# One token load ahead of two transposing DMAs, the last scales later, one copy ahead of a square

## The chip, the cores and the metric

The kernel runs on one core of one Trainium2 chip. The metric is the device time of one execution in microseconds (us), of which a profiled execution also gives the span from the first to the last instruction. Five engines work side by side, each through its own instructions in order: TensorE (PE, matmuls; PEld its weight loads), VectorE (DVE), ScalarE (ACT), GpSimd (POOL) and SyncE (SP, which here only issues DMAs).

## The reference

Attention over 4 batches, 8 heads, 576 tokens and 64 features (four heads with a plain window of 32, four with a dilated one), then two dense layers over its 2304 tokens:

```python
h = x @ w_in                      # 2304x512 @ 512x2048
y = (h - tanh(h)) @ w_out         # -> 2304x512

h = y @ w_in2                     # 2304x512 @ 512x1024
e = exp(h - max(h, axis=-1))
solu = h * (e / (sum(e) + 1e-9))
mu, var = mean(solu), mean((solu - mu) ** 2)
out = ((solu - mu) / sqrt(var + 1e-6) * g_ln) @ w_out2     # 1024 -> 512
```

All of it is in float32; the kernel forms products from a high and a low half of each operand.

## The kernel before

The program has three parts. Attention and the first dense layer go first, in groups of 384 tokens. The first layer's output y goes to a DRAM buffer `y_dr`. The second layer, which all of the change concerns, reads it back in nine **pairs** (0 to 8) of 256 tokens, that is 18 **tiles** of 128 tokens: pair p has tiles 2p and 2p+1, and the odd one is finished first.

For each pair, `load_y(j)` (L636) loads y from DRAM into a buffer `yr`; SP issues it. There are two buffers of this kind, one that the even pairs 2, 4, 6, 8 take in turn and one for the odd pairs from 3 on. `split_y` makes PE's input of it, in parts: part "r" scales `yr` in place on ACT (L644) with `ysc`, part "s" makes sums and differences of quarters on POOL (L652), and parts 0, 2 and 1 round to float16 (on DVE at L664, or on ACT at L662 where `act=True`) and leave the remainder to POOL (L665).

`mm3(i)` is the first product of pair i, put together from seven block products of 6 matmuls each (`prod`, L749, a scheme with fewer block products than the plain one): "b11", "t2", "t1", "t3", "t4", "b21", "b22", in this order, in four PSUM banks. ACT copies the first bank to `c` (L781). DVE adds the second bank and `c` to `u2` (L784), the fourth bank and `u2` to `u3` (L792), and `neg_add` (L764) makes the scaled, negated h with a running minimum. "t4" is written into the second bank, so it waits until `u2` is made; "b21" goes into the fourth bank, so it waits for `u3`. `softmax_e` (L820, ACT) takes the exponential, `softmax_u` (L825) and `softmax_z` (L831, L832) on DVE make the product and take off the mean, `square` (L841, ACT) and `fac` (L846, L847, POOL) give the factor of the tile. `split_z` rounds to float16 (L869, ACT) and takes the remainder (L870, DVE); a transposing DMA (L874, issued by SP) turns the result, for tiles 1 and 17 PE does it (`trz`). `mm4` is the second product, 24 matmuls for a tile (L897); its result is scaled on ACT (L900) and stored (L901). `rest`, `rest1` and `rest2` make the scale that L900 needs.

PE's order is mm3(0), mm3(1), mm4 of tiles 1 and 0, mm3(2), mm4 of tiles 3 and 2, mm3(3) and so on: the work of ACT, DVE and POOL on pair i goes on while PE does mm4 of pair i-1. What is issued when is written out by hand: `mm3` calls functions that are given to it (`mid`) at four places, and `first` to `fourth` are those of pairs 1 and 2. All engines take their instructions in the order in which these lines are called.

`y_scale(k)` makes the scales of three pairs at a time from the maxima `ym`. For k = 0 and 1 it runs within the first layer; `y_scale(2, ...)` gives the scales of pairs 6, 7 and 8, its second half is `scale2`, called in `fourth`.

Of the kernel before, what the change touches and what calls it, by code (L numbers as in the profile page):

```python
# [14 lines left out]
ALU = mybir.AluOpType  # L15
# [25 lines left out]
def tile_kernel(ctx: ExitStack, tc: tile.TileContext, qk, vw, cst, w_in, w_out, w_in2, w_out2, g_ln, out):  # L41
    nc = tc.nc
# [38 lines left out]
    wsc = const.tile([128, 8], F32, name="wsc")  # L81
# [170 lines left out]
    def y_scale(k, pool, tag):  # L252

        d = ysc[:, k]
        m = ym[:, 2 * k:2 * k + 2]
        ps = spread(m, pool, tag, f"ysp{k}")

        def far():
            nc.vector.tensor_reduce(out=m, in_=ps, axis=mybir.AxisListType.X, op=ALU.max)

        def then():
            if k < 2:
                far()
            for c, a, b in ((0, 0, 0), (1, 0, 1), (2, 1, 1)):
                nc.vector.tensor_scalar(out=d[:, 0, c:c + 1], in0=m[:, a:a + 1], scalar1=m[:, b:b + 1], scalar2=2.0 ** -100,
                                        op0=ALU.max, op1=ALU.max)
            nc.vector.reciprocal(out=d[:, 1], in_=d[:, 0])
            nc.vector.tensor_scalar(out=d[:, 1], in0=d[:, 1], scalar1=2.0 ** 13, scalar2=None, op0=ALU.mult)
            nc.vector.tensor_scalar(out=d[:, 2], in0=d[:, 0], scalar1=wsc[:, 3:4], scalar2=-(2.0 ** -16), op0=ALU.mult,
                                    op1=ALU.mult)  # L270
        return then if k < 2 else (far, then)

# [359 lines left out]
    def load_y(j):  # L632
        if j < NP:
            pool = p3 if j > 2 and j % 2 else p2
            y_raw[j] = pool.tile([128, KD, YT], F32, tag="yr", name=f"yr{j}", bufs=1)
            nc.sync.dma_start(out=y_raw[j], in_=y_dr[:, :, j * YT:(j + 1) * YT])  # L636

    def split_y(j, parts=range(3), act=False):

        if j >= NP:  # L640
            return
        r = y_raw[j]
        if "r" in parts:
            nc.scalar.activation(out=r, in_=r, func=AF.Copy, scale=ysc[:, j // 3, 1, j % 3:j % 3 + 1])  # L644
        if 0 in parts:
            yt[j] = p2.tile([128, 2, 7, 2, TT], F16, tag="yt", name=f"yt{j}")
        if 0 in parts and j not in y_sm or "s" in parts:
            sm = y_sm[j] = p2.tile([128, 3, 2, TT], F32, tag="ysm", name=f"ysm{j}", bufs=1)
            a11, a21, a22 = r[:, 0:2, 0:TT], r[:, 0:2, TT:YT], r[:, 2:4, TT:YT]
            for o, a, b, op in ((sm[:, 0], a21, a22, ALU.add), (sm[:, 1], sm[:, 0], a11, ALU.subtract),  # L650
                                (sm[:, 2], a11, a21, ALU.subtract), (a21, r[:, 2:4, 0:TT], sm[:, 1], ALU.subtract)):
                nc.gpsimd.tensor_tensor(out=o, in0=a, in1=b, op=op)  # L652
        if not set(parts) & {0, 1, 2}:
            return
        y, sm = yt[j], y_sm[j]
        yh = y[:, 0].rearrange("p s k t -> p (s k) t")
        yl = y[:, 1].rearrange("p s k t -> p (s k) t")
        for p, sl, v in ((0, slice(0, 4), r[:, :, 0:TT]), (2, slice(4, 8), r[:, :, TT:YT]),
                         (1, slice(8, 14), sm.rearrange("p s k t -> p (s k) t"))):
            if p in parts:  # L660
                if act:
                    nc.scalar.copy(out=yh[:, sl], in_=v)  # L662
                else:
                    nc.vector.tensor_copy(out=yh[:, sl], in_=v)  # L664
                nc.gpsimd.tensor_tensor(out=yl[:, sl], in0=v, in1=yh[:, sl], op=ALU.subtract)  # L665
        if 2 in parts:
            y_raw.pop(j)
            y_sm.pop(j)
# [84 lines left out]
    def bank(pool, tag, i, nm):  # L753
        return pool.tile([128, 512], F32, tag=tag, name=f"s{nm}_{i}")
# [12 lines left out]
    def mm3(i, mid=()):  # L767

        y = yt.pop(i)
        sm = sml[i] = p3.tile([128, 2, 8], F32, tag="sml", name=f"sml{i}", bufs=3)  # L770
        for t in range(2):
            st[2 * i + t] = dict(sml=sm[:, t])
        mid = dict(mid)
        b0, b1 = bank(sa, "b0", i, "p1"), bank(sa, "b1", i, "p6")
        prod(b0, y, 0, "b11")
        prod(b1, y, 5, "t2")
        u2 = p3.tile([128, 512], F32, tag="u2", name=f"u2_{i}", bufs=1)
        u3 = p3.tile([128, 512], F32, tag="u3", name=f"u3_{i}", bufs=1)
        b2, b3 = bank(sb, "b2", i, "p5"), bank(sb, "b3", i, "p7")
        c = p3.tile([128, 512], F32, tag="c", name=f"c_{i}", bufs=1)  # L780
        nc.scalar.copy(out=c, in_=b0)  # L781
        if i > 0:
            split_y(i + 2, ("r",))
        nc.vector.tensor_tensor(out=u2, in0=b1, in1=c, op=ALU.add)  # L784
        if i > 2:
            split_y(i + 1, (1, 2))
            load_y(i + 3)
        prod(b2, y, 4, "t1")
        if 0 in mid:
            mid[0]()  # L790
        prod(b3, y, 6, "t3")
        nc.vector.tensor_tensor(out=u3, in0=b3, in1=u2, op=ALU.add)  # L792
        neg_add(i, 1, 1, b2, u3)
        b1 = bank(sa, "b1", i, "p4")
        prod(b1, y, 3, "t4")
        neg_add(i, 1, 0, b1, u3)
        if 1 in mid:
            mid[1]()
        softmax_e(2 * i + 1)
        b3 = bank(sb, "b3", i, "p2")  # L800
        prod(b3, y, 1, "b21")
        neg_add(i, 0, 0, b3, c)
        softmax_u(2 * i + 1)
        if 2 in mid:
            mid[2]()
        prod(b2, y, 2, "b22", first=False)
        neg_add(i, 0, 1, b2, u2)
        if 3 in mid:
            mid[3]()
        softmax_e(2 * i)  # L810
        softmax_z(2 * i + 1)
        square(2 * i + 1)
        fac(2 * i + 1)
        softmax_u(2 * i)
        softmax_z(2 * i)

# [20 lines left out]
    def square(i):  # L837

        d = st[i]
        d["f"], d["g"] = d["sml"][:, 4:5], d["sml"][:, 6:7]  # L840
        nc.scalar.activation(out=d["e"], in_=d["hn"], func=AF.Square, accum_out=d["sml"][:, 5:6])  # L841

    def fac(i):

        sc, var = (st[i]["sml"][:, c:c + 1] for c in (4, 5))
        nc.gpsimd.tensor_scalar(out=var, in0=var, scalar1=2.0 ** -20 / FF2, scalar2=1e-37, op0=ALU.mult, op1=ALU.max)  # L846
        nc.gpsimd.tensor_tensor(out=sc, in0=var, in1=half, op=ALU.pow)  # L847
# [12 lines left out]
    def rest2(p):  # L860
        ssum, sc, var, g = (sml[p][:, :, c] for c in (1, 4, 5, 6))
        nc.vector.tensor_tensor(out=var, in0=var, in1=sc, op=ALU.mult)
        nc.vector.scalar_tensor_tensor(out=g, in0=ssum, scalar=wsc[:, 6:7], in1=var, op0=ALU.mult, op1=ALU.mult)  # L863

    def split_z(i, dma=True):

        d = st[i]
        ab = d["ab"] = d["e"].bitcast(F16).rearrange("p (a n) -> p a n", a=2)
        nc.scalar.activation(out=ab[:, 0], in_=d["hn"], func=AF.Copy, scale=d["f"])  # L869
        nc.vector.scalar_tensor_tensor(out=ab[:, 1], in0=d["hn"], scalar=d["f"], in1=ab[:, 0], op0=ALU.mult,  # L870
                                       op1=ALU.subtract)
        t = d["zt"] = p3.tile([128, 2, NF2, TT], F16, tag="zt", name=f"zt{i}", bufs=4)
        if dma:
            nc.sync.dma_start_transpose(out=t.rearrange("p a j t -> p (a j) t"), in_=ab.rearrange("p a n -> p (a n)"))  # L874
# [29 lines left out]
    y_rows(2)  # L904
    split_y(2, ("r", "s"))
    mm3(0)
    far, scale2 = y_scale(2, zo, "zp")
    far()
# [12 lines left out]
    def third():  # L921
        rest2(0)
        split_y(2, act=True)

    def fourth():
        rest2(1)
        scale2()
        split_y(3, act=True)
        load_y(5)

    mm3(1, {0: first, 1: second, 3: third})
    for i in range(NP):
        o, e = 2 * i + 3, 2 * i + 2
        last = i + 2 == NP
        if i + 1 < NP:
            square(e)
            fac(e)
            split_z(o, not last)
            if i > 0:
                rest(i + 1)  # L940
            split_z(e)
            if i > 0:
                split_y(i + 3, (0,))
                rest1(i + 1)
            if last:
                rest2(i + 1)
            if i == 0:
                load_y(4)
        mm4(2 * i + 1)
        mm4(2 * i, (lambda: trz(o)) if last else None)  # L950
        if i == 0:
            mm3(2, {0: lambda: split_y(3, ("s",)), 1: lambda: (rest(1), rest1(1)), 3: fourth})
        elif i + 2 < NP:
            mm3(i + 2, {3: lambda: rest2(i + 1)})
# [77 lines left out]
```

## Time and profile before

| | us |
|---|---|
| median of 3 runs | 701.3 (699.94 to 701.52) |
| profiled execution | 700.27 |
| its span | 698.5 |
| PE busy | 673.4 |
| DVE busy | 501.3 |
| ACT busy | 384.2 |
| POOL busy | 172.9 |

PE is the engine that works nearly all the time. The others have much free time on the whole, so the place of their waits matters and not their sum. In the rows below a line of a timeline gives the start and the duration in us, the engine, the line of the kernel, the operation, what it writes and reads with shapes, and how many instructions are merged in it; in brackets stands how long the engine stood idle just before, and what ended that.

### The profile page before, as it was taken

The page shows a single profiled execution, that of the slowest core. Times are in us where ns is not written, and L with a number is a line of the kernel's source. Part 1 is how long each engine was busy: PE and PEld are TensorE (multiplying, and loading weights), DVE is VectorE, ACT ScalarE, POOL GpSimd, SP SyncE. Part 2 cuts the span into 40 slices and gives each one's busy share as a digit, 9 for nine tenths or more (in the row PEclk, how much of TensorE's full clock was granted, in tenths as well). Part 3 has the DMA queues.
Part 4 walks back from the last instruction along what each step waited for, and adds up shares of the span by engine and source line. Part 5 has one row for each costly group of instructions (what it writes and reads, how often), then busy time and mean ns, then how long its engine had stood idle before and what let it go on. Part 6 is the DMA issues. An engine that isn't in the chain of part 4 may idle for free. (4 is left out here: it accounts for less than half of the span.)

```text
span 698.5 us, 11389 instructions
## 1 busy us (share of the span) xinstructions
PE 673.4 (96%) x4010; PEld 558.9 (80%) x4010; DVE 501.3 (72%) x1257; ACT 384.2 (55%) x917; POOL 172.9 (25%) x174
## 2 busy tenths in 40 slices
PE   6898999999999999999999999999999969999997
PEld 5687899999999999999999999999944424444443
DVE  5987667477767876787777743599978577777751
ACT  5778776455555555455555533475657345555442
POOL 2312311101110111101111010365225456545410
PEclk9999999999999999999999999999999989999999
DMA  9975641242334332342213001453311554433243
GB/s 281 349 252 177 192 123 23 95 143 90 116 121 139 103 115 91 121 155 87 82 53 114 2 1 60 165 178 134 114 46 30 131 140 103 80 97 78 70 88 92
DMA packets 68009, 80.82 MB, mean 116 GB/s; under 512 B 36592, under 2 KB 52464, under 8 KB 67952
## 3 DMA queue, kind: packets, MB, share of 16 engines
q1 hardware_dynamic: 64784, 75.37, 36.6%
q10 hardware_dynamic: 3168, 4.72, 1.8%
q8 instruction: 32, 0.52, 0.3%
q14 instruction: 25, 0.20, 0.1%
HBM read 62.25 MB, written 9.44 MB: 103 GB/s over the span
## 5 line engine op out<-in xcount | busy, mean ns | idle before, releaser
L458 PE MATMUL h<-x,wi 128*128 128x384 f32 x1152 | 221.8, 342 | 1.1 <-DVE t L469 1.1
L485 PE MATMUL y<-gs,wo 128*128 128x384 f32 x1152 | 217.7, 339 | 0.0
L458 PEld LDWEIGHTS h<-x,wi 128*128 128x128 f32 x1152 | 199.7, 190 | 2.4 <-DVE t L469 1.3
L485 PEld LDWEIGHTS y<-gs,wo 128*128 128x128 f32 x1152 | 199.6, 189 | 1.8
L357 POOL TENSOR_TENSOR p<-p,rs 96x512 f32<-96x512 f32 x47 | 57.5, 1222 | 352.2 <-DVE rs L355 307.6
L475 DVE TENSOR_TENSOR gs<-t,gs 128x384 fp32r<-128x384 f32 x96 | 81.4, 848 | 24.3 <-ACT gs L472 24.2
L469 DVE TENSOR_TENSOR t<-h,t 128x384 f32<-128x384 f32 x96 | 53.0, 552 | 63.0 <-ACT t L466 62.8
L897 PE MATMUL po<-w2o_o,zt 128*128 128x512 f16 x432 | 95.1, 379 | 0.6 <-DVE zt L886 0.6
L466 ACT ACTIVATE t<-h 128x384 f32<-128x384 f32 x96 | 46.8, 488 | 82.8 <-PE h L458 79.3
L349 ACT ACTIVATE p<-p,nm 96x128 f32<-96x128 f32 x192 | 75.0, 393 | 21.2 <-DVE nm L314 20.8
L472 ACT CAST gs<-t 128x384 fp32r<-128x384 f32 x96 | 48.9, 510 | 63.8 <-DVE t L469 63.6
L897 PEld LDWEIGHTS <-zt 128*128 128x128 f16 x432 | 42.1, 98 | 51.8 <-DVE zt L886 1.1
L749 PEld LDWEIGHTS <-yt 128*128 128x128 f16 x378 | 37.4, 99 | 53.8 <-issue 11.3
L749 PE MATMUL sp<-w2i_t,yt 128*128 128x512 f16 x216 | 49.8, 386 | 7.7 <-DVE u L784 7.7
L820 ACT ACTIVATE e<-hn,sml 128x1024 f32<-128x1024 f32 x18 | 20.7, 1148 | 53.8 <-DVE sml L764 40.6
L870 DVE SCALAR_TENSOR_TENSOR e<-hn,sml,e 128x1024 f16<-128x1024 f32 x18 | 25.6, 1425 | 19.0 <-ACT e L869 19.0
L749 PE MATMUL sp<-w2i_b,yt 128*128 128x512 f16 x162 | 38.7, 384 | 0.0
L309 PE MATMUL qkp<-qkr 64*96 64x128 f32 x160 | 29.4, 339 | 7.1 <-DMA qkr<-in_qk_dram 5.4
L349 ACT ACTIVATION_READ_ACCUMULATOR p<-p,nm 96x1 f32 x192 | 36.2, 189 | 0.0
L309 PEld LDWEIGHTS qkp<-qkr 64*96 64x96 f32 x160 | 24.1, 205 | 11.7 <-DMA qkr<-in_qk_dram 5.7
L396 DVE TENSOR_TENSOR x<-pv,x 128x384 fp32r<-128x384 f32 x24 | 16.2, 697 | 20.2 <-ACT x L394 19.8
L364 PE MATMUL tp<-cst_sb,p 96*128 96x96 f32 x192 | 27.0, 268 | 3.4 <-POOL p L357 2.4
(111 smaller groups left out, 825.2 us busy)
## 6 DMA issues: line engine op xcount, KB each, us to landing
qkr<-in_qk_dram SPq DMA_DIRECT2D x28, 448.0 KB, 3.4
raw_wi<-in_w_in_dram SPq DMA_DIRECT2D x16, 511.8 KB, 7.1
raw_wo<-in_w_out_dram SPq DMA_DIRECT2D x16, 511.8 KB, 7.3
v<-in_vw_dram SPq DMA_DIRECT2D x48, 128.0 KB, 3.4
y_dr<-ys ACTq DMA_DIRECT2D x6, 768.0 KB, 3.9
yr<-y_dr SPq DMA_DIRECT2D x9, 512.0 KB, 5.1
out_dram<-o SPq DMA_DIRECT2D x18, 256.0 KB, 2.7
qkr<-in_qk_dram SPq DMA_DIRECT2D x20, 224.0 KB, 5.3
```

What stands on the lines that cost most here:

```text
L309: nc.tensor.matmul(ps[:, b], d["r"][:64, b * NQ:(b + 1) * NQ], d["r"][:64, QC + b * NK:QC + (b + 1) * NK], start=True, stop=True)
L349: nc.scalar.activation(out=d["p"][:, b], in_=d["p"][:, b], func=AF.Exp, scale=-1.0, bias=d["nm"][:, b:b + 1], accum_out=d["sm"][:, b:b + 1])
L357: eng.tensor_tensor(out=d["p"], in0=d["p"], in1=d["rs"].unsqueeze(2).to_broadcast([NQ, 4, NK]), op=ALU.mult)
L364: nc.tensor.transpose(ps[:NK, b * NQ:(b + 1) * NQ], d["p"][:, b], ident[:NQ, :NQ])
L458: nc.tensor.matmul(ps, w[:, a, k * 128:(k + 1) * 128], xt[g, k][:, b], start=(n == 0), stop=(n == 3 * KD - 1))
L466: nc.scalar.activation(out=t, in_=ps, func=AF.Tanh)
L469: nc.vector.tensor_tensor(out=t, in0=ps, in1=t, op=ALU.subtract)
L472: nc.scalar.copy(out=gs[:, 0], in_=t)
L475: nc.vector.tensor_tensor(out=gs[:, 1], in0=t, in1=gs[:, 0].bitcast(F32), op=ALU.subtract)
L485: nc.tensor.matmul(yb[g][m], wo[c][:, a, m * 128:(m + 1) * 128], gs[:, b], start=(c == 0 and i == 0), stop=(c == NF - 1 and i == 2))
L749: nc.tensor.matmul(ps, y[:, a, blk, kk], w2i[w, kk][:, b], start=first and q == 0, stop=q == 5, skip_group_check=not first)
L897: nc.tensor.matmul(po, z[:, a, j], w2o[j][:, b], start=(q == 0), stop=(q == 3 * NF2 - 1))
```

## The change

`load_y(4)` is called ahead of the two `split_z` of pair 1 in place of behind them. `y_scale` makes its nine values with four DVE instructions in place of six, and `scale2` moves from `fourth` (in mm3(2)) to the place behind `rest1(2)`. In mm3(0) `square(1)` and `fac(1)` fall away at the end, and mm3(1) calls them behind its copy to `c`; the scaling of y of pair 3, which stood there, moves to the end of `third`. For the last pair `rest2(8)` moves behind `trz(17)`.

```diff
@@ y_scale
         def then():
             if k < 2:
                 far()
-            for c, a, b in ((0, 0, 0), (1, 0, 1), (2, 1, 1)):
-                nc.vector.tensor_scalar(out=d[:, 0, c:c + 1], in0=m[:, a:a + 1], scalar1=m[:, b:b + 1], scalar2=2.0 ** -100,
-                                        op0=ALU.max, op1=ALU.max)
+            nc.vector.tensor_scalar(out=d[:, 0, 0:3:2], in0=m, scalar1=2.0 ** -100, scalar2=2.0 ** -13, op0=ALU.max,
+                                    op1=ALU.mult)
+            nc.vector.tensor_tensor(out=d[:, 0, 1:2], in0=d[:, 0, 0:1], in1=d[:, 0, 2:3], op=ALU.max)
             nc.vector.reciprocal(out=d[:, 1], in_=d[:, 0])
-            nc.vector.tensor_scalar(out=d[:, 1], in0=d[:, 1], scalar1=2.0 ** 13, scalar2=None, op0=ALU.mult)
-            nc.vector.tensor_scalar(out=d[:, 2], in0=d[:, 0], scalar1=wsc[:, 3:4], scalar2=-(2.0 ** -16), op0=ALU.mult,
+            nc.vector.tensor_scalar(out=d[:, 2], in0=d[:, 0], scalar1=wsc[:, 3:4], scalar2=-(2.0 ** -3), op0=ALU.mult,
                                     op1=ALU.mult)
@@ mm3
         nc.scalar.copy(out=c, in_=b0)
-        if i > 0:
+        if i == 1:
+            square(1)
+            fac(1)
+        if i > 1:
             split_y(i + 2, ("r",))
...
         softmax_e(2 * i)
         softmax_z(2 * i + 1)
-        square(2 * i + 1)
-        fac(2 * i + 1)
+        if i > 0:
+            square(2 * i + 1)
+            fac(2 * i + 1)
@@ the order of the second layer
     def third():
         rest2(0)
         split_y(2, act=True)
+        split_y(3, ("r",))
 
     def fourth():
         rest2(1)
-        scale2()
         split_y(3, act=True)
         load_y(5)
...
             square(e)
             fac(e)
+            if i == 0:
+                load_y(4)
             split_z(o, not last)
             if i > 0:
                 rest(i + 1)
@@
                 split_y(i + 3, (0,))
                 rest1(i + 1)
-            if last:
-                rest2(i + 1)
-            if i == 0:
-                load_y(4)
+            if i == 1:
+                scale2()
         mm4(2 * i + 1)
-        mm4(2 * i, (lambda: trz(o)) if last else None)
+        mm4(2 * i, (lambda: (trz(o), rest2(i + 1))) if last else None)
```

SP's queue at the beginning of the second layer, before (the numbers behind `yr`, `zt` and `e` are pair and tile):

```order
L636 DMA yr3_5706<-y_dr_86 128x4x256
L874 DMA_TRANSPOSE zt0_5870<-e0_5782 128x16x128
L874 DMA_TRANSPOSE zt3_5919<-e3_5876 128x16x128
L874 DMA_TRANSPOSE zt2_5923<-e2_5904 128x16x128
L636 DMA yr4_5925<-y_dr_86 128x4x256
```

The same place in the changed kernel:

```order
L635 DMA yr3_5702<-y_dr_86 128x4x256
L877 DMA_TRANSPOSE zt0_5865<-e0_5778 128x16x128
L635 DMA yr4_5913<-y_dr_86 128x4x256
L877 DMA_TRANSPOSE zt3_5917<-e3_5871 128x16x128
L877 DMA_TRANSPOSE zt2_5921<-e2_5900 128x16x128
```

The load of pair 4 has moved past the transposes of tiles 3 and 2, and stands behind that of tile 0.

DVE from the last product of tile 5 to `u2` of pair 3, before; the four lines with `ysc` are `scale2`:

```order
L265 TENSOR_SCALAR ysc_96<-ym_95 128x1 x3
L267 RECIPROCAL ysc_96<-ysc_96 128x3
L268 TENSOR_SCALAR ysc_96<-ysc_96 128x3
L269 TENSOR_SCALAR ysc_96<-ysc_96,wsc_93 128x3
L831 TENSOR_SCALAR sml2_5983<-sml2_5983 128x1
L832 TENSOR_SCALAR hn5_6024<-hn5_6024,sml2_5983 128x1024
...
L870 SCALAR_TENSOR_TENSOR e4_6074<-hn4_6047,sml2_5983,e4_6074 128x1024
L664 CAST yt4_6098<-yr4_5925 128x512
L784 TENSOR_TENSOR u2_3_6178<-sp6_3_6165,c_3_6182 128x512
L664 CAST yt4_6098<-yr4_5925 128x512
L664 CAST yt4_6098<-ysm4_6099 128x768
L792 TENSOR_TENSOR u3_3_6179<-sp7_3_6181,u2_3_6178 128x512
```

The end of that stretch in the changed kernel:

```order
L873 SCALAR_TENSOR_TENSOR e4_6064<-hn4_6043,sml2_5979,e4_6064 128x1024
L663 CAST yt4_6088<-yr4_5913 128x512
L264 TENSOR_SCALAR ysc_96<-ym_95 128x2
L266 TENSOR_TENSOR ysc_96<-ysc_96 128x1
L267 RECIPROCAL ysc_96<-ysc_96 128x3
L268 TENSOR_SCALAR ysc_96<-ysc_96,wsc_93 128x3
L786 TENSOR_TENSOR u2_3_6172<-sp6_3_6159,c_3_6176 128x512
L663 CAST yt4_6088<-yr4_5913 128x512
L663 CAST yt4_6088<-ysm4_6089 128x768
L794 TENSOR_TENSOR u3_3_6173<-sp7_3_6175,u2_3_6172 128x512
```

`scale2` has gone from ahead of `softmax_z` of tile 5 to the place directly ahead of `u2` of pair 3.

ACT at the end of mm3(0) and the start of mm3(1), before:

```order
L820 ACTIVATE e0_5782,sml0_5718<-hn0_5772,sml0_5718 128x1024
L841 ACTIVATE e1_5763,sml0_5718<-hn1_5753 128x1024
L781 COPY c_1_5815<-sp1_1_5797 128x512
L644 ACTIVATE yr3_5706<-yr3_5706,ysc_96 128x1024
L869 ACTIVATE e1_5763<-hn1_5753,sml0_5718 128x1024
```

And in the changed kernel:

```order
L823 ACTIVATE e0_5778,sml0_5714<-hn0_5768,sml0_5714 128x1024
L780 COPY c_1_5808<-sp1_1_5790 128x512
L844 ACTIVATE e1_5759,sml0_5714<-hn1_5749 128x1024
L872 ACTIVATE e1_5759<-hn1_5749,sml0_5714 128x1024
```

The copy to `c` of pair 1 has moved past the square of tile 1, and the scaling of `yr3` is no longer between the square and tile 1's `split_z`.

## Rows read from the trace of the kernel before

**Rows 1.** Timeline of PE around mm3(3), mm3(4) and mm3(5):

```profile
556.96 1.46 PE L749 MATMUL sp<-w2i_b,yt 128*128 128x512 f16 x6
...
569.25 2.72 PE L749 MATMUL sp<-w2i_t,yt 128*128 128x512 f16 x6 [6.95 <-DVE u L784]
...
585.46 1.46 PE L749 MATMUL sp<-w2i_b,yt 128*128 128x512 f16 x6
...
604.88 1.46 PE L749 MATMUL sp<-w2i_b,yt 128*128 128x512 f16 x6
```

**Rows 2.** Stretch: us, busy (x) PE, PEld, DVE, ACT, POOL; PEclk, DMA, GB/s:

```profile
557.00:585.50 28.50, 21.55 (x92) 9.30 (x91) 22.05 (x39) 14.57 (x21) 16.27 (x20) 0.88 0.38 93
```

**Rows 3.** Timeline of ACT, from mm3(1) to mm3(2):

```profile
530.81 1.15 ACT L820 ACTIVATE e<-hn,sml 128x1024 f32<-128x1024 f32 x1 [1.81 <-DVE sml L764]
...
550.64 1.15 ACT L644 ACTIVATE yr<-yr,ysc 128x1024 f32<-128x1024 f32 x1 [9.21 <-DMA yr<-y_dr]
551.69 1.13 ACT L820 ACTIVATE e<-hn,sml 128x1024 f32<-128x1024 f32 x1
```

**Rows 4.** Timeline of SP's queue, 525 to 570 us:

```profile
527.79 17.07 SPq L874 DMA_TRANSPOSE zt<-e  x3
544.95 0.92 SPq L636 DMA_DIRECT2D yr<-y_dr  x1
```

**Rows 5.** The tile yr from 500 to 600 us, its loads:

```profile
DMA to landing us min/median/max: 4.0/4.1/5.7
```

**Rows 6.** Timeline of POOL, three remainders of split_y (pairs 2, 3, 4):

```profile
532.13 1.64 POOL L665 TENSOR_TENSOR yt<-ysm,yt 128x768 f16<-128x768 f32 x1
...
556.26 1.64 POOL L665 TENSOR_TENSOR yt<-ysm,yt 128x768 f16<-128x768 f32 x1
...
568.74 1.16 POOL L665 TENSOR_TENSOR yt<-yr,yt 128x512 f16<-128x512 f32 x1 [1.69 <-DVE yt L664]
```

**Rows 7.** Timeline of DVE, from pair 1's end to mm3(3):

```profile
532.29 2.03 DVE L832 TENSOR_SCALAR hn<-hn,sml 128x1024 f32<-128x1024 f32 x1
...
538.75 3.31 DVE L870 SCALAR_TENSOR_TENSOR e<-hn,sml,e 128x1024 f16<-128x1024 f32 x2 [2.31 <-ACT e L869]
...
544.40 0.81 DVE L764 CUSTOM_DVE_ANT_0 hn<-sp,u,sml 128x512 f32<-128x512 f32 x1
...
556.25 0.44 DVE L265 TENSOR_SCALAR ysc<-ym 128x1 f32<-128x1 f32 x3
...
556.93 0.99 DVE L268 TENSOR_SCALAR ysc<-ysc 128x3 f32<-128x3 f32 x1
...
558.15 0.75 DVE L832 TENSOR_SCALAR hn<-hn,sml 128x1024 f32<-128x1024 f32 x1
...
568.18 0.41 DVE L664 CAST yt<-yr 128x512 f16<-128x512 f32 x1
...
569.12 1.06 DVE L664 CAST yt<-yr 128x512 f16<-128x512 f32 x1
...
570.57 0.68 DVE L792 TENSOR_TENSOR u<-sp,u 128x512 f32<-128x512 f32 x1
```

**Rows 8.** Timelines of ACT, DVE and PE at mm3(1):

```profile
519.64 0.56 ACT L781 COPY c<-sp 128x512 f32<-128x512 f32 x1
...
521.18 0.68 DVE L784 TENSOR_TENSOR u<-sp,c 128x512 f32<-128x512 f32 x1
...
521.92 1.46 PE L749 MATMUL sp<-w2i_t,yt 128*128 128x512 f16 x6 [0.75 <-DVE u L784]
```

**Rows 9.** Timelines of DVE and PE at the last pair:

```profile
683.80 0.22 DVE L863 SCALAR_TENSOR_TENSOR sml<-sml,wsc 128x2 f32<-128x2 f32 x1 [0.52 <-POOL sml L858]
...
684.68 10.10 PE L897 MATMUL po<-w2o_o,zt 128*128 128x512 f16 x46 [0.61 <-DVE zt L886]
```

**Rows 10.** Stretches at the start of the first layer, columns as in rows 2:

```profile
57.50:61.20 3.70, 1.49 (x11) 1.40 (x11) 2.68 (x13) 3.30 (x13) 1.91 (x1) 1.00 0.91 260
61.30:64.60 3.30, 3.30 (x12) 3.30 (x11) 3.26 (x8) 3.05 (x7) 1.91 (x1) 0.50 0.20 82
```

## The prediction

> **What bounds the kernel now.** I began with the page: PE is busy almost throughout, so time can only be won where PE stands idle or runs at the lower clock. The chain that ended last showed only the final 26 us, so I went on to the waits by sum, restricted to the second layer, where the edits lie. PE waits there for DVE at three places, and each has an edit beside it. I then read each engine's timeline around these places.
>
> The large one is in mm3(3). A pair costs PE 90 matmuls, and from mm3(4) to mm3(5) that is 604.88 - 585.46 = 19.42 us without a gap [rows 1]. From mm3(3) to mm3(4) it is 585.46 - 556.96 = 28.50 us. Of the 9.08 us between them 6.95 are the idle time that `u2` ended [rows 1]. The other 2.13 are lost to the clock: the mean granted clock of the stretch is 0.88 [rows 2], so part of the matmuls behind the gap ran at 1.2 GHz and not at 2.4.
>
> Why was `u2` late? ACT stood 9.21 us in front of the scaling of `yr4`, until the load landed; only then came the exponential of tile 5, at 551.69 [rows 3]. All of DVE's later work on pair 2 follows from it. Its input had been made by 544.40 + 0.81 = 545.21 [rows 7]. The load was issued only at 544.95, behind three transposes that held SP's queue for 17.07 us from 527.79 [rows 4], and landed 5.7 us later [rows 5]. The reader should see that the transfer is short; it stood in the wrong place of a queue.
>
> **The load.** In the new order it waits for the buffer alone, which POOL gives back with its remainders of pair 2, at the latest at 532.13 + 1.64 = 533.77 [rows 6]. With 4.0 to 5.7 us to landing [rows 5] it is there by 537.8 to 539.5. ACT wants it at 550.64 - 9.21 = 541.43 [rows 3], so that wait goes. While SP waits for the buffer, the transposes of tiles 3 and 2 stand behind it; their inputs are made by two instructions that start at 538.75 [rows 7], so nothing is delayed there. The scaling itself, 1.15 us, then ends near 542.6, well ahead of the exponential, which can start at about 545.25, 6.44 us sooner than at 551.69.
>
> **What is late next.** I move DVE's row of `u3` of pair 3 by this: it ended at 570.57 + 0.68 = 571.25 [rows 7], so 564.81. Taking `scale2` out of the chain ahead of tile 5's `softmax_z` gives less than its place of 556.25 to 558.15. POOL is in a remainder until 557.90 [rows 6], and the same DVE instruction beside the same POOL work of pair 2 took 2.03 us in place of 0.75 and ended at 534.32, 0.55 behind POOL's end [rows 6, 7]. So I expect 557.90 + 0.55 = 558.45 for an end that was 558.90: 0.45 won, `u3` at 564.36. The bounds are nothing, and 1.8 if POOL does not hold it.
>
> PE needs `u3` after 30 matmuls of mm3(3); at 19.42 / 90 = 0.2158 us each that is 556.96 + 6.47 = 563.43. So even without `scale2` about 0.9 us of the gap stays: pair 2 is the one pair whose rounding of the next y stands on ACT and POOL amid its own softmax.
>
> Now `scale2` stands right ahead of `u2`. Its four instructions cost 0.15 to 0.22 us each if nothing holds them (three took 0.44 [rows 7]), some 0.7 together. But one of the old ones took 0.99 us and ended with POOL's remainder (556.93 + 0.99 = 557.92 against 557.90 [rows 6, 7]). In the new place POOL begins a remainder right behind the cast, at 568.74 for 1.16 us [rows 6]. I take one instruction held until it ends, at 569.90 in the old frame, which puts `u2` 1.5 us later. The cast behind `u2` took 1.06 in place of 0.41 beside this same remainder [rows 7]; that 0.65 comes back, since POOL's work is then over. With small overlaps `u3` is about 1.05 later. The gap that stays in mm3(3) is 0.93 + 1.05 = 2.0 us. Its bounds: 0, if POOL holds neither `softmax_z` nor `scale2` (the 1.35 of the first more than covers the rest); 2.9, if POOL's next instruction holds one more of the four.
>
> The Trainium skill, page "SBUF — State Buffer", section "SBUF: two separate sides", says that VectorE and GpSimd share one pair of ports as an exclusive lock, and that a VectorE instruction with two SBUF inputs takes part in it. By that rule the new maximum of two columns, a tensor-tensor, is an instruction that can be held, where the three it replaces can hardly be; the row of 0.44 for three beside POOL agrees, and the sum by it would be the 2.9 above.
>
> **Copy c, square and yr3.** PE's 0.75 us in mm3(1) ended with `u2`, which DVE began at 521.18 with no idle time ahead, 0.98 us behind the end of the copy at 520.20 [rows 8]. DVE's own queue was the limit, so an earlier copy gives nothing. It pushes tile 1's square back by up to 0.56 [rows 8], and with it the chain through POOL, ACT and DVE to PE's transposes of tile 1, which follow directly. Less the scaling of `yr3` that is no longer between, I take a loss of 0.2, from 0 to 0.5. The scaling, 1.15 us, fits into the 1.81 that ACT stood idle ahead of tile 2's exponential [rows 3]; without that cover it would cost at most 1.15.
>
> **The end.** PE waits 0.61 us for the copy of tile 17's transposed half, which stands behind `rest2`, which itself waited 0.52 for POOL [rows 9]. Behind the copy, `rest2` is needed only when mm4 of tile 17 ends, several us later. I take the whole 0.6; the bounds are 0 and 0.61.
>
> The two instructions saved for k = 0 and 1 lie under the first layer's matmuls, which PE does back to back there; uncovered, two by about 0.15 to 0.99 each.
>
> **The sum.** 698.5 - 6.95 - 2.13 + 2.0 + 0.2 - 0.6 = 691.0 us of span. The profiled execution has 1.77 us around its span, so 692.8. It is 1.0 below the median of the three runs and 0.5 below the mean of all four; I add this 0.5 and forecast 693.3.
>
> **Rivals.** (1) The clock falls again. A gap of some 2 us can be enough: in the first layer, after a stretch in which PE was busy for 1.49 of 3.70 us, the clock stood at 1.2 GHz for 3.3 us [rows 10]; after 0.75 us [rows 8] it did not. Half of 3.3 is 1.7 us: 695.0. (2) Nothing is left in mm3(3), because POOL and DVE do not meet: 693.3 - 2.0 = 691.3. For it: PE has no gap there in the later pairs; against: those pairs don't have pair 2's work on POOL. (3) The lock holds one instruction more, a gap of 2.9: 694.2. (4) The load is still late, or what it released is held by something else: 6.95 and the clock stay, 700. It would need a landing 2 us past the slowest of rows 5. (5) Slower: each of the four instructions at the pinch is held as long as the 2.03 row. Then the gap is 0.9 + 8.1 = 9.0 us, the clock falls as before (2.13), and the span is 689.0 + 9.0 + 2.13 = 700.1, 1.6 over the span before. It decides from a gap of about 7.4 us on; against it, no row shows two instructions in a row held so long.
>
> **How the numbers follow.** The forecast, with a gap between 0.9 and 2.5, has 0.58; (1) 0.18; (2) 0.12; (3) 0.08; (4) and (5) 0.02 each. The likeliest gives 693.3. The range of 691.0 to 695.8 takes in (1) to (3) with some 0.5 for the spread of the runs, and leaves out 0.04 and the worst of (1) together with (3). A change under 0.2%, 1.4 us, can't be told from none by these runs: faster 0.96, same 0.02, slower 0.02.
>
> **What would show it.** After the change the scaling of `yr4` should start without a wait for a DMA, near 541.5 to 542; the exponential of tile 5 near 545.5; PE's gap in mm3(3) should be around 2 us and split between `u2` and `u3`; `scale2` should hold one instruction of near 1 us; the gap of 0.75 should still be in mm3(1); that of 0.61 should be gone. I am wrong if another wait than `scale2` or POOL holds pair 2, or if mm3(1) loses more than 0.5 us.

## The result and the profile after

| | before | changed |
|---|---|---|
| median, us | 700.62 (699.14 to 701.52, 4 runs) | 691.62 (691.25 to 692.85, 4 runs) |
| profiled execution, us | 700.27 | 692.85 |
| its span, us | 698.5 | 691.1 |
| PE busy, us | 673.4 | 671.4 |

The ratio is 0.9877, with a 95% interval of 0.9853 to 0.99: the change makes the kernel 1.2% faster. The profiled executions differ by 7.4 us, the medians by 9.0. By the stages below the second layer gives 7.6 us. The changed kernel was run beside the kernel before twice more (e6 and e10 below), and there the medians differ by 7.0 and 7.2 us. What moves a time by 1 to 2 us from one execution to the next is taken up at the end.

For the second layer it is best to measure stages by PE: from the first matmul of one mm3 to the first of the next, as PE's timeline gives them. A stage between two pairs without any wait is 19.42 us. Times in us, for the kernels of this study:

| kernel | mm3(1) to mm3(2) | mm3(2) to mm3(3) | mm3(3) to mm3(4) | mm3(8) to the last matmul's end |
|---|---|---|---|---|
| before | 21.57 | 19.57 | 28.50 | 31.62 |
| changed | 22.15 | 19.57 | 21.12 | 30.85 |
| the load alone (e1) | 21.56 | 19.59 | 20.88 | 31.63 |
| all but the load (e2) | 22.16 | 19.57 | 30.38 | 30.84 |
| square ahead again (e3) | 21.44 | 19.58 | 21.10 | 30.84 |
| last scales later (e4) | 22.12 | 19.59 | 20.42 | 30.85 |
| both (e5) | 21.42 | 19.57 | 20.44 | 30.84 |
| both, rounding sooner (e7) | 21.42 | 19.59 | 19.42 | 30.85 |
| both, maximum later (e8) | 21.45 | 19.57 | 20.43 | 30.84 |

PE's timeline of the changed kernel in mm3(1) and mm3(3), where [rows 1] and [rows 8] showed gaps of 6.95 and 0.75 us:

```profile
522.09 1.46 PE L748 MATMUL sp<-w2i_t,yt 128*128 128x512 f16 x6 [0.76 <-DVE u L786]
523.38 0.61 PE L885 MATMUL zp<-id,e 128*128 128x128 f16 x8
524.41 0.62 PE L885 MATMUL zp<-id,e 128*128 128x128 f16 x8 [0.42 <-DVE e L873]
...
557.71 1.46 PE L748 MATMUL sp<-w2i_b,yt 128*128 128x512 f16 x6
559.01 4.05 PE L748 MATMUL sp<-w2i_t,yt 128*128 128x512 f16 x18
564.48 1.46 PE L748 MATMUL sp<-w2i_t,yt 128*128 128x512 f16 x6 [1.42 <-DVE u L786]
```

The gap of 6.95 has become one of 1.42. The one of 0.75 is still there, and 2.3 us behind it a new one of 0.42 has come. A gap behind a matmul of 512 columns costs 0.16 us more than its row says: the row counts from the end of the matmul ahead, 0.38 us behind that one's start, while without a wait the next matmul starts 0.22 us behind it.

The stretches of mm3(3) and mm3(4) in the changed kernel (columns as in rows 2):

```profile
557.70:578.80 21.10, 19.68 (x91) 8.78 (x90) 17.44 (x34) 10.75 (x16) 12.14 (x14) 1.00 0.46 101
578.80:598.20 19.40, 19.40 (x91) 8.82 (x90) 15.73 (x30) 9.80 (x14) 10.86 (x14) 1.00 0.46 108
```

The granted clock is 1.00 in both, where [rows 2] had 0.88: with the long gap the fall to 1.2 GHz behind it is gone as well.

SP's queue in the changed kernel, and under it ACT at mm3(2):

```profile
528.54 2.10 SPq L877 DMA_TRANSPOSE zt<-e  x1
532.95 0.54 SPq L635 DMA_DIRECT2D yr<-y_dr  x1
541.18 4.36 SPq L877 DMA_TRANSPOSE zt<-e  x2
```

```profile
541.61 0.59 ACT L780 COPY c<-sp 128x512 f32<-128x512 f32 x1
542.07 1.17 ACT L643 ACTIVATE yr<-yr,ysc 128x1024 f32<-128x1024 f32 x1
546.01 1.15 ACT L823 ACTIVATE e<-hn,sml 128x1024 f32<-128x1024 f32 x1 [2.77 <-DVE sml L763]
```

The load is issued 12 us sooner than in [rows 4], in a time when SP waited anyway, and the transposes that it passed leave the queue at 541.18 + 4.36 = 545.54, 0.68 later than in [rows 4] (544.86), while PE begins mm3(2) 0.75 later: nothing is lost there. The scaling of `yr4` follows the copy without a wait, where [rows 3] had 9.21 us. ACT now waits for DVE, as it should: the exponential starts when its input is made.

### The profile page after: what moved, and what is told of

Its sections match the earlier page's. It is cut to its first block, busy times and chain, and to the rows that moved or that the text cites. A ratio compares the mean times of both kernels' runs of the same rounds, so it can differ in the third digit from the quotient of the medians.

```text
span 691.1 us, 11384 instructions
## 1 busy us (share of the span) xinstructions
PE 671.4 (97%) x4010; PEld 558.3 (81%) x4010; DVE 501.5 (73%) x1251; ACT 384.3 (56%) x917; POOL 173.3 (25%) x174
## 5 line engine op out<-in xcount | busy, mean ns | idle before, releaser
L484 PE MATMUL y<-gs,wo 128*128 128x384 f32 x1152 | 217.9, 339 | 0.0
L484 PEld LDWEIGHTS y<-gs,wo 128*128 128x128 f32 x1152 | 199.8, 189 | 1.8
L823 ACT ACTIVATE e<-hn,sml 128x1024 f32<-128x1024 f32 x18 | 20.7, 1149 | 56.3 <-DVE sml L763 43.5
L308 PE MATMUL qkp<-qkr 64*96 64x128 f32 x160 | 29.5, 339 | 7.3 <-DMA qkr<-in_qk_dram 5.5
L308 PEld LDWEIGHTS qkp<-qkr 64*96 64x96 f32 x160 | 24.1, 205 | 11.8 <-DMA qkr<-in_qk_dram 5.9
```

The source lines that it names most:

```text
L308: nc.tensor.matmul(ps[:, b], d["r"][:64, b * NQ:(b + 1) * NQ], d["r"][:64, QC + b * NK:QC + (b + 1) * NK], start=True, stop=True)
L484: nc.tensor.matmul(yb[g][m], wo[c][:, a, m * 128:(m + 1) * 128], gs[:, b], start=(c == 0 and i == 0), stop=(c == NF - 1 and i == 2))
```

## The experiments

Three theories stood against each other. Mine: the place of the load is nearly all of the gain, the last scales cost something at their new place, and the earlier copy costs something too. The first rival: taking the scales off tile 5's chain is needed for the gain. The second: the earlier copy saves something in mm3(1).

**e1_load_alone.** The kernel before, and the load ahead of the two `split_z`:

```diff
             square(e)
             fac(e)
+            if i == 0:
+                load_y(4)
             split_z(o, not last)
...
-            if i == 0:
-                load_y(4)
```

> The kernel before with the load of pair 4 moved and nothing else. My theory (the load's place is nearly all of the gain): ACT's wait of 9.21 us for the load is gone, the exponential of tile 5 starts some 6.4 us sooner, PE's delay in mm3(3) falls from 6.95 plus the clock to about 1.4 us in sum, the gaps of 0.75 in mm3(1) and 0.61 at the end stay. Time about 7.7 us under before, within 1 us of the changed kernel. Rival (the scales' move off tile 5's chain is needed too): PE still waits 4 us or more in mm3(3), and time is 4 us or more over the changed kernel's.

Measured: 691.84 us, ratio to before 0.9898 (0.9871 to 0.9926), 7.9 us under the kernel before that ran beside it. The changed kernel's ratio is 0.9877, so this one edit is the gain as far as the runs can tell. PE's timeline in mm3(3):

```profile
557.43 4.05 PE L749 MATMUL sp<-w2i_t,yt 128*128 128x512 f16 x18
562.03 1.45 PE L749 MATMUL sp<-w2i_t,yt 128*128 128x512 f16 x6 [0.55 <-DVE u L784]
564.08 2.75 PE L749 MATMUL sp<-w2i_b,yt 128*128 128x512 f16 x12 [0.59 <-DVE u L792]
```

Two small waits are left, for `u2` and then for `u3`. The stage is 20.88 us, 1.46 over 19.42, against 1.4 expected; the first rival asked for 4 or more and falls. The stage is even 0.24 us shorter than in the changed kernel.

**e2_all_but_load.** The changed kernel with the load put back behind the transposes:

```diff
-            if i == 0:
-                load_y(4)
             split_z(o, not last)
...
             if i == 1:
                 scale2()
+            if i == 0:
+                load_y(4)
```

> The changed kernel with the load of pair 4 put back behind the transposes. My theory: ACT waits 9 us for the load again, PE stands about 7 us in mm3(3) and the clock falls behind it, time within 1.5 us of before. Rival (the smaller edits bring a good part): PE's gap in mm3(3) is 5 us or less and time is 2 us or more under before.

Measured: 700.27 us, ratio to before 1.0009 (0.9984 to 1.0033): no gain. ACT's row, then PE's:

```profile
551.70 1.15 ACT L643 ACTIVATE yr<-yr,ysc 128x1024 f32<-128x1024 f32 x1 [9.46 <-DMA yr<-y_dr]
```

```profile
571.17 2.72 PE L748 MATMUL sp<-w2i_t,yt 128*128 128x512 f16 x6 [8.06 <-DVE u L786]
573.69 4.26 PE L748 MATMUL sp<-w2i_b,yt 128*128 128x512 f16 x12
```

The wait for the DMA is back, and PE's gap is 8.06 us where 7 were expected, 1.1 longer than in [rows 1]. DVE's rows say why: `scale2` now stands between the late tile 4 and `u2`, which starts 1.65 us behind the start of the cast ahead of it (0.34 in the kernel before). The stage is 30.38 us, 10.96 over 19.42: 8.2 for the gap, and 2.7 behind it, where the matmuls run at the lower clock. Six matmuls take 2.72 us here and 1.46 in the changed kernel.

**e3_square_ahead.** The changed kernel with the order of square and copy as before:

```diff
-        if i == 1:
-            square(1)
-            fac(1)
         if i > 1:
             split_y(i + 2, ("r",))
...
-        if i > 0:
-            square(2 * i + 1)
-            fac(2 * i + 1)
+        square(2 * i + 1)
+        fac(2 * i + 1)
```

> The changed kernel with tile 1's square ahead of the copy c again (the scaling of yr3 stays at its later place). My theory: PE's wait of 0.42 us ahead of the second half of tile 1's transposes is gone, the wait for u2 in mm3(1) stays 0.75, so PE starts mm3(2) about 0.4 us sooner, counted from mm3(1). Rival (the earlier copy is worth something): u2 of pair 1 starts later and PE's wait for it grows by 0.3 us or more.

Measured: 692.28 us in one execution, and a stage of 21.44 us in place of 22.15. PE in mm3(1):

```profile
522.23 1.46 PE L748 MATMUL sp<-w2i_t,yt 128*128 128x512 f16 x6 [0.76 <-DVE u L783]
523.53 1.06 PE L881 MATMUL zp<-id,e 128*128 128x128 f16 x16
```

The wait for `u2` is 0.76 with the copy late or early, and the transposes are one group of 16 again. So the copy was never what `u2` waited for, the rival falls, and the copy's move costs 0.71 us, more than the 0.4 expected. Against before the stage is 0.13 shorter. The scaling of `yr3` is the edit that lies there (the load alone leaves the stage at 21.56): ACT begins `split_z` of tile 1 5.19 us behind the stage's start in place of 5.33. That this is what moving the scaling gave is read from these rows; it was not tried alone.

**e4_scale2_later.** The changed kernel with the last scales within mm3(3):

```diff
-            if i == 1:
-                scale2()
...
-            mm3(i + 2, {3: lambda: rest2(i + 1)})
+            mm3(i + 2, {3: lambda: (rest2(i + 1), scale2() if i == 1 else None)})
```

> The changed kernel with the last scales behind rest2(2) within mm3(3), where POOL is idle. My theory: the four instructions take 0.7 us in sum there, and PE's delay in mm3(3) falls from 1.7 us (30 matmuls then take 6.47 us plus that) to about 0.9, since the cast behind u2 is held by POOL in their place. Rival (the scales at that place cost nothing, since what they wait for holds the next instruction anyway): the delay in mm3(3) stays at 1.5 us or more. A second rival: it falls to 0.3 or less.

Measured: 691.17 us in one execution. DVE's rows:

```profile
561.32 0.68 DVE L786 TENSOR_TENSOR u<-sp,c 128x512 f32<-128x512 f32 x1
561.92 1.06 DVE L663 CAST yt<-yr 128x512 f16<-128x512 f32 x1
...
569.39 0.16 DVE L264 TENSOR_SCALAR ysc<-ym 128x2 f32<-128x2 f32 x1
...
569.88 0.20 DVE L268 TENSOR_SCALAR ysc<-ysc,wsc 128x3 f32<-128x3 f32 x1
```

The last of the four takes 0.20 us where POOL is idle. The stage is 20.42 us, 1.00 over 19.42 and 0.70 less than in the changed kernel; and the cast behind `u2` takes 1.06 us again, held in their place, as expected. The delay of 1.00 was expected at 0.9, and both rivals (1.5 or more, 0.3 or less) fall.

**e5_three_edits** is e3 and e4 together.

> The changed kernel with both of the edits that cost something put elsewhere: tile 1's square ahead of the copy again, the last scales behind rest2(2) in mm3(3). My theory: the two gains add up, PE's wait of 0.42 in mm3(1) is gone and its delay in mm3(3) is about 0.8 us in place of 1.7, so it is 1.3 us under the changed kernel (0.2%), near the limit of what runs can tell. Rival: one gain eats the other, and at most 0.5 us are left in the trace.

Measured: 691.87 us, ratio to before 0.9887 (0.9869 to 0.9905). The stages are 21.42 and 20.44 us: the two gains add up in the trace, 1.4 us. The delay in mm3(3) is 1.02, a little over the 0.8 expected. The changed kernel ran again beside it:

**e6_changed_again.**

> The changed kernel again, beside the others on the same chip, so that differences of 1 to 2 us can be told. Expected 691 to 693 us, with the same waits as in its first trace.

Measured: 692.86 us, ratio 0.9901 (0.9881 to 0.9922), with stages of 22.13 and 21.08. The medians differ by 1.0 us and the intervals overlap, so the runs alone don't show the 1.4.

**e7_rounding_sooner.** e5, and POOL's remainder of pair 3 is got out of the way of tile 5's `softmax_z`. `rest`, `rest1` and `rest2` of pair 1 move too:

```diff
+            if i == 1:
+                rest(1)
+                rest1(1)
             square(e)
             fac(e)
+            if i == 1:
+                rest2(1)
...
-            mm3(2, {0: lambda: split_y(3, ("s",)), 1: lambda: (rest(1), rest1(1)), 3: fourth})
+            mm3(2, {0: lambda: split_y(3, ("s",)), 1: lambda: split_y(3, act=True), 3: lambda: load_y(5)})
```

> As e5_three_edits, and the rounding of y of pair 3 moves ahead of tile 5's exponential, so that POOL is done with it before softmax_z of tile 5; rest, rest1 and rest2 of pair 1 move to the time when DVE waits for tile 4's factor. My theory (POOL's remainder of pair 3 holds softmax_z and is the rest of the delay): the 128x1024 instruction of tile 5 takes 0.75 us in place of 2.03, and PE's delay in mm3(3) falls to 0.2 us or less. Rival (DVE is late for another reason): the instruction is short, but the delay stays over 0.5 us, or the remainder holds another instruction just as long.

Measured: 689.32 us in one execution. DVE's two rows of tile 5, and PE's of mm3(3):

```profile
545.43 1.86 DVE L824 SCALAR_TENSOR_TENSOR hn<-hn,e 128x1024 f32<-128x1024 f32 x1 [0.27 <-ACT e L819]
...
548.13 0.76 DVE L831 TENSOR_SCALAR hn<-hn,sml 128x1024 f32<-128x1024 f32 x1
```

```profile
555.86 1.46 PE L748 MATMUL sp<-w2i_b,yt 128*128 128x512 f16 x6
557.15 5.34 PE L748 MATMUL sp<-w2i_t,yt 128*128 128x512 f16 x24
562.33 2.75 PE L748 MATMUL sp<-w2i_b,yt 128*128 128x512 f16 x12
```

The 128x1024 instruction takes 0.76 us in place of 2.03. POOL's remainder now runs beside the product ahead of it, which takes 1.86 us in place of 1.23, but that is the cheaper meeting. PE has no gap in mm3(3), and the stage is 19.42 us like all later ones. The end of this instruction comes 2.06 us sooner, counted from the start of mm3(3), than in e5, and only 1.28 of that are its own. Ahead of it in e5 stood the two instructions of `rest2(1)`, 0.38 and 1.01 us beside the same POOL work, which e7 moves away (they take 0.16 and 0.22 there). So what was left of the delay is this stretch of DVE beside POOL's rounding; how much is due to the rounding's new place and how much to the three moved calls was not told apart.

**e8_far_later.** e5, and the maximum that stood on DVE ahead of `u2` of pair 1 goes behind it:

```diff
-    far()
 
     def first():
+        far()
         split_z(1, False)
```

> As e5_three_edits, and the maximum over the spread rows for the last scales (0.42 us on DVE directly ahead of u2 of pair 1) moves behind u2. My theory (DVE's own queue and not the copy c sets u2 there): u2 starts 0.3 to 0.4 us sooner and PE's wait in mm3(1) falls from 0.75 to about 0.4. Rival (the copy sets it): the wait stays at 0.7 or more.

Measured: 691.25 us in one execution. PE in mm3(1):

```profile
521.55 1.46 PE L748 MATMUL sp<-w2i_t,yt 128*128 128x512 f16 x6 [0.43 <-DVE u L783]
522.84 1.27 PE L881 MATMUL zp<-id,e 128*128 128x128 f16 x16
```

The wait falls from 0.75 to 0.43, so DVE's own queue does set `u2`. But the stage is 21.45 us against 21.42: the transposes of tile 1 now take 1.27 in place of 1.06 us, since the remainder that they read is no sooner made (DVE begins it 6.38 us behind the stage's start, 6.35 in e5). A wait that is shown shorter is not time won; this one only moved.

**e9_rounding_timed** is e7's kernel, timed, beside the changed kernel on the same chip (**e10_changed_third**).

> The same kernel as e7_rounding_sooner, timed. My theory: with no delay left in mm3(3) the stage takes 19.4 us, 1.7 less than in the changed kernel, and mm3(1) 0.7 less, so the time is about 2.4 us (0.35%) under the changed kernel run beside it, some 689.5 us. Rival (what is won in these stages is lost elsewhere, or drowned by the spread): the two medians are within 1 us.

> The changed kernel, beside e9_rounding_timed on the same chip. Expected 691.5 to 693 us with a stage of 21.1 us from mm3(3) to mm3(4).

Measured: 690.68 us (ratio to before 0.9869, 0.9845 to 0.9892) against 692.82 (0.9887, 0.9866 to 0.9908), with stages of 21.42 and 19.42 against 22.14 and 21.09. The medians differ by 2.1 us, the stages by 2.4, so the rival (within 1 us) falls; the median is 1.2 us over the 689.5 expected. It is the best version of this study by the sum of its stages; that it beats the changed kernel is shown by the trace and not by the intervals, which overlap.

## Why the prediction was right, point by point

The sum gave 691.0 us of span and 692.8 for a profiled execution; they were 691.1 and 692.85. The mechanism of the large term is right. That the sum fits to 0.1 us is luck in part, since the errors of the small terms cancel: the delay in mm3(3) is 0.30 less than forecast, mm3(1) loses 0.38 more, the end gives 0.17 more, and PE comes to mm3(1) 0.17 later.

Of the signs named beforehand two failed. The gap in mm3(3) is not split between `u2` and `u3`: PE stands 1.42 us for `u2`, and no row shows it waiting for `u3`. And mm3(1) lost 0.58 us, over the 0.5 from which the prediction called itself wrong.

**The load** was right in mechanism and size. It was issued at 532.95 (533.77 at the latest was predicted), the scaling started at 542.07 (541.5 to 542), and the exponential of tile 5 at 546.01 (545.5, and the stage was 0.75 late). e1 and e2 show that it alone makes the gain, and that without it there is none. Of the 9.08 us the sum put 6.95 to the gap and 2.13 to the clock; with the 0.16 that the gap's row leaves out they are 7.11 and 1.97, and the sum stays.

**The delay that stays in mm3(3)** was put at 2.0 us and measured 21.12 - 19.42 = 1.70. Its two parts were 0.93 without `scale2` and 1.05 for `scale2` at its new place. e4, which has `scale2` elsewhere, leaves 1.00, and the place costs 0.70. The 1.05 is the part that was mis-sized: 1.5 less the 0.65 that comes back is 0.85, and the 0.2 on top was not worked out. The lower bound of 0 also left out that the four instructions take 0.7 us when nothing holds them; with that it is 0.3. DVE in the changed kernel, and POOL beside it:

```profile
549.17 0.38 DVE L865 TENSOR_TENSOR sml<-sml 128x2 f32<-128x2 f32 x1
549.65 1.01 DVE L866 SCALAR_TENSOR_TENSOR sml<-sml,wsc 128x2 f32<-128x2 f32 x1
...
550.76 2.03 DVE L835 TENSOR_SCALAR hn<-hn,sml 128x1024 f32<-128x1024 f32 x1
...
562.09 0.42 DVE L663 CAST yt<-yr 128x512 f16<-128x512 f32 x1
562.43 0.16 DVE L264 TENSOR_SCALAR ysc<-ym 128x2 f32<-128x2 f32 x1
562.62 0.16 DVE L266 TENSOR_TENSOR ysc<-ysc 128x1 f32<-128x1 f32 x1
562.82 0.18 DVE L267 RECIPROCAL ysc<-ysc 128x3 f32<-128x3 f32 x1
562.91 0.92 DVE L268 TENSOR_SCALAR ysc<-ysc,wsc 128x3 f32<-128x3 f32 x1
563.75 0.68 DVE L786 TENSOR_TENSOR u<-sp,c 128x512 f32<-128x512 f32 x1
564.34 0.41 DVE L663 CAST yt<-yr 128x512 f16<-128x512 f32 x1
```

```profile
550.61 1.64 POOL L664 TENSOR_TENSOR yt<-ysm,yt 128x768 f16<-128x768 f32 x1
...
562.65 1.15 POOL L664 TENSOR_TENSOR yt<-yr,yt 128x512 f16<-128x512 f32 x1 [1.69 <-DVE ysc L264]
```

The instruction of `softmax_z` was held as predicted: 2.03 us, its end 0.54 behind POOL's. One of the four scale instructions was held until POOL's remainder ended (563.83 against 563.80), and the cast behind `u2` gave its 0.65 back (0.41 in place of 1.06). By the stages of e1 and of the changed kernel the scales' move and shortening cost 0.24 us in sum: off the old place 0.46 are won (20.88 against 20.42 in e4; 0.45 was forecast), and the new one costs 0.70 against a place where POOL is idle (e4).

**The lock rule.** The Trainium skill, page "SBUF — State Buffer", section "SBUF: two separate sides", says that of a VectorE and a GpSimd instruction that both need the shared ports the one that starts first goes through and the other waits. The rows don't speak against it: the new tensor-tensor began at 562.62, 0.03 us ahead of POOL, and took 0.16. In the other traces with this order (e2, e3, e6, e10) it began 0.03 to 0.04 ahead too. The rival of 2.9 us did not come; by this rule it hung on those 0.03 us, and no run here made it start later, so the rule is not tested by them. What was held is the 128x3 instruction that reads `ysc` and `wsc`, and not the reciprocal of the same size (0.18).

**Copy c** is the term that failed in size: 0.2, with 0.5 as its bound, against 22.15 - 21.57 = 0.58 measured, of which the move is 0.71 and the scaling of `yr3` gave back 0.13 (e3). The step "it pushes tile 1's square back by up to 0.56" took the chain behind it as fixed, and it counted too much for the scaling of `yr3`, most of whose 1.15 us lay under ACT's wait for POOL (0.80 us in e3). POOL's two instructions of that chain, in the changed kernel and then in e3:

```profile
520.47 0.73 POOL L849 TENSOR_SCALAR sml<-sml 128x1 f32<-128x1 f32 x1 [8.48 <-ACT e L844]
521.28 0.57 POOL L850 TENSOR_TENSOR sml<-sml,half 128x1 f32<-128x1 f32 x1
```

```profile
520.14 0.23 POOL L845 TENSOR_SCALAR sml<-sml 128x1 f32<-128x1 f32 x1 [8.00 <-ACT e L840]
520.45 0.84 POOL L846 TENSOR_TENSOR sml<-sml,half 128x1 f32<-128x1 f32 x1
```

Counted from the stage's start the first comes 0.47 us later. It then met DVE's 128x1024 `softmax_z` of tile 0 (520.36 to 521.11) and took 0.73 us in place of 0.23, while the second, which stands beside that DVE instruction in e3, took 0.57 in place of 0.84. In sum the chain is 0.70 later, which is the 0.71 of the stage. That the meeting holds them was argued from these rows and not tried apart.

**The end** gave 31.62 - 30.85 = 0.77 us, against 0.6 with 0.61 as its bound: the mechanism was right, and the bound was the gap of the row, without the 0.16. PE's rows there in the changed kernel have no gap:

```profile
674.65 1.06 PE L885 MATMUL zp<-id,e 128*128 128x128 f16 x16
675.55 11.82 PE L900 MATMUL po<-w2o_o,zt 128*128 128x512 f16 x54
```

**The clock** was the rival with the highest chance, 0.18, and it stayed at 1.00 behind the gap of 1.42 us.

**The median** was forecast at 693.3 and came out at 691.62, 1.7 lower, inside the range. I had carried the spread of before over as it was and added 0.5, but here the profiled execution was the longest of the four. Three of the four had a mean clock of 1.000 and spans of 689.5, 689.5 and 690.1 us; the profiled one had 0.998 and 691.1, and its trace shows the clock falling once in the first layer, as in the profile of before [rows 10]. The edits don't touch that part. The four were short ones: the later medians of the same kernel are 692.86 (e6) and 692.82 (e10), 0.5 under the forecast.

## What to carry to other kernels

A DMA that waits on its queue behind others is as late as their inputs are, however short its own transfer: look where its issue stands, and move it ahead of those that wait longer. When a long wait goes, price what is late next by moving the old rows along the chain, with the work on other engines that they will meet; here that gave the remainder within 0.3 us. A wait of PE that ends with an engine's instruction is worth an edit only if that instruction can start sooner by it and if what PE needs next is not late anyway. The earlier copy did not let `u2` start sooner, and it made what came next later by 0.71 us. The later maximum shortened the wait by 0.32 us, and PE stood as much longer behind it.

## What the runs showed of the hardware

A long gap of PE cost more than itself, since the matmuls behind it ran at the lower clock: behind 8.06 us of idle PE (e2, mean granted clock of the stage 0.83) 2.7 us were lost, behind 6.95 (before, 0.88) 2.0, behind 1.42 (changed, 1.00) none.

The same gap of 2.2 us in the first layer was followed by a fall in some executions and not in others. The changed kernel (a fall) and e5 (none), each with the stretch around the gap and the one behind it:

```profile
57.60:61.10 3.50, 1.28 (x9) 1.12 (x9) 2.71 (x13) 3.10 (x13) 1.91 (x1) 1.00 0.96 274
61.20:64.50 3.30, 3.30 (x12) 3.30 (x11) 3.11 (x7) 3.06 (x7) 1.91 (x1) 0.50 0.23 92
```

```profile
60.10:64.00 3.90, 1.66 (x12) 1.63 (x12) 2.88 (x13) 3.50 (x13) 1.91 (x1) 1.00 0.95 283
64.10:67.40 3.30, 3.30 (x21) 3.05 (x20) 3.27 (x8) 3.07 (x7) 1.91 (x1) 1.00 0.13 51
```

The code of this part is the same in both; in the second the clock stood at 2.4 GHz behind the gap, and 21 matmuls began in 3.3 us in place of 12. From the first matmul of L484 behind the gap to the next of L308 PE took 5.92 us with the fall and 4.35 without: some 1.6 us of a time can hang on this, more than most of the edits here are worth. Of the twelve traces seven have the fall and five (e1, e4, e5, e7, e10) have not, with the kernel before in the first group and the changed one in both; what decides it was not found. Nor is it all that varies: the changed kernel in e10 has no fall and still 691.3 us of span, since PE came to the same matmuls ahead of the gap 2 us later than in the first trace (45.5 us in place of 43.5).

Where short instructions of DVE and POOL meet long ones of the other, they can cost several times their own time: 0.92 us for 128x3 on DVE, 0.73 for 128x1 on POOL, each around 0.2 when alone, and each ended within 0.1 us behind the other engine's instruction. Not all are held: three of 128x1 took 0.44 us together beside POOL [rows 7], and the reciprocal of 128x3 took 0.18.
